# Sliding-window attention and a SwiGLU block on one core: attention ended at block 4, block 5's gate and value by seven products, sums on GpSimd

## The chip, the cores and the metric

The kernel runs on one core of a Trainium2 chip. A core has a matrix engine (PE), a vector engine (DVE), a scalar engine (ACT), GpSimd (POOL) and a queue engine (SP); all work from an on-chip memory (SBUF) and PE writes its products to eight banks of PSUM. Each engine runs its own instructions in order and waits on semaphores for the others. The metric is the time of one execution in device microseconds, lower is better; three runs of the kernel before gave 333.97, 334.12 and 334.51.

## What is computed

Eight batches of eight heads, 576 positions, head size 64: attention in a causal window of 128 with a linear distance bias, then a gated feed-forward block on the 4608 tokens.

```python
scores = scale * np.matmul(q, k.transpose(0, 1, 3, 2))
mask = (rel >= 0) & (rel < window)
scores = np.where(mask, scores + bias[None], -1000000000.0)
...
attn = attn / (np.sum(attn, axis=-1, keepdims=True) + 1e-09)
return np.matmul(attn, v).astype(np.float32)
...
g = x @ w_gate
silu = g * (1.0 / (1.0 + np.exp(-g)))
val = x @ w_val
return (silu * val @ w_out).astype(np.float32)
```

x is the attention output with the heads side by side: 4608 x 512; w_gate and w_val are 512 x 1536, w_out is 1536 x 512.

## The kernel before

**Attention** is cut into 36 units of 128 queries, nine for each pair of batches (four of the first batch, four of the second, and one that holds the last 64 rows of both). Unit i needs rank i of k and q, transposed to kT (12 slots) and qT (9 slots), and v. POOL's queue issues the loads (L184, L190; five buffers each for k and q), unit i loading rank i + 7; SP's queue issues the DMA transposes (L238), up to four ranks ahead. Scores go to banks of ps_a (L291, L327; tag "a", four banks), ACT takes exp (L297, L331), DVE multiplies by the bias mask (L303, L335; two inputs in SBUF). `weighted` multiplies by v into two more ps_a banks (av, L359); DVE takes the reciprocal of the row sums (L362) and divides into the tile x (L363; pool xpool, three buffers). `x_transposed` transposes x into xT of its block by a DMA of SP (L381); xT has three buffers for blocks 0 to 7, and block 8 (the 64-row remainders) has its own. A block is 512 tokens, so four units fill one xT: units 18 to 21 block 4, 22 to 25 block 5, 27 to 30 block 6, 31 to 34 block 7; every ninth unit (8, 17, 26, 35) goes to block 8.

**The feed-forward part** goes block by block, 0 to 8. Gate and value come classically in blocks 0 to 5: for each of 12 groups of 128 columns four matmuls of 512 columns for the gate and four for the value (L415), in the three banks "gv" of ps_f. ACT takes tanh of half the gate (L433), DVE forms (tanh + 1) x gate (uu, L434) and multiplies by the value (hT, L445). From block 6 on (`SEVEN_FROM`) gate and value are made by seven products of half-size matrices, Strassen's scheme in Winograd's form: a unit of two column groups takes seven products of four 256-column matmuls (L639), in ps_a banks gX and gY and a "gv" bank gZ; the weights' sums (T1 to T4 of a unit, L613 to L616) and x's sums (S1 to S4, L503 to L506) are made beforehand by DVE. They lie in SBUF that attention no longer needs: slots of kT and qT, and the masks. Silu comes there from ACT directly (L661, L692); DVE adds (L676, L684) and multiplies (L677, L693).

The projection by w_out (L550) goes by seven products too, in blocks 1 to 8, two halves of seven parts of six matmuls each; its parts of block n - 1 are interleaved with the gates and values of block n. The sums of hT that it needs come from the same four instructions (L503 to L506).

**Order.** The program is written as two generators, attention and feed-forward, that `everything` interleaves: from step 60 on, attention has a target of `84 + (step - 57) * RATE / 34.5` of its own steps, 34.5 steps being one block. PE's order is then as written out; DVE's and ACT's is set by a scheduler; POOL's and, from unit 12 on, SP's queue are as written. In block 5, when column group 7 (`SILU_AT`) is done, `attention_ends` runs what is left of attention and makes ACT load the table of Silu; column groups 8 to 11 of block 5 then use Silu directly (`by_silu`), and the weight sums for the seven products begin.

Of the kernel before, what the change touches and what calls it, by code (L numbers as in the profile page):

```python
# [11 lines left out]
FP16 = mybir.dt.float16  # L12
# [17 lines left out]
FIRST = 4  # L30
LEAD = 6
PRE = 0
SEVEN_FROM = 6
SILU_AT = 7
SECOND = 5.5
RATE = 54.0
FIXED_FROM = 60
LATE = 13


def slot(h):
# [11 lines left out]
def kernel(  # L53
# [366 lines left out]
        return ps  # L420

    acted = {}
    by_silu = set()

    def gate(n, m, pg, c0=0, c1=512):

        if (n, m) not in acted:
            acted[(n, m)] = [supool.tile([P, 512], FP16, name=i, tag=i) for i in ("tt", "uu")]
        tt, uu = (t_[:, c0:c1] for t_ in acted[(n, m)])
        if (n, m) in by_silu:  # L430
            nc.scalar.activation(tt, pg[:, c0:c1], AF.Silu)
            return
        nc.scalar.activation(tt, pg[:, c0:c1], AF.Tanh, scale=0.5)  # L433
        nc.vector.scalar_tensor_tensor(out=uu, in0=tt, scalar=one if (n, m) == PIN else 1.0,  # L434
                                       in1=pg[:, c0:c1], op0=ALU.add, op1=ALU.mult)

    def val(n, m, pv, c0=0, c1=512):

        if n not in hT:
            hT[n] = hpool.tile([P, NMB, 512], FP16, name="hT", tag="hT")  # L440
        if (n, m) in by_silu:
            nc.vector.scalar_tensor_tensor(out=hT[n][:, m, c0:c1], in0=acted[(n, m)][0][:, c0:c1], scalar=2.0,
                                           in1=pv[:, c0:c1], op0=ALU.mult, op1=ALU.mult)
            return
        nc.vector.tensor_mul(hT[n][:, m, c0:c1], acted[(n, m)][1][:, c0:c1], pv[:, c0:c1])  # L445
# [52 lines left out]
    one_more = []  # L498
    hsum = {}

    def four_sums(a11, a12, a21, a22, s2, s3, s4):

        return [lambda: nc.vector.tensor_sub(s3, a11, a21),  # L503
                lambda: nc.vector.tensor_add(a21, a21, a22),
                lambda: nc.vector.tensor_sub(s2, a21, a11),
                lambda: nc.vector.tensor_sub(s4, a12, s2)]  # L506

    def at_once(fs):
        for f in fs:
            f()  # L510

    def sums(n, c):

        if n not in hsum:
            hsum[n] = [spool.tile([P, HM, 256], FP16, name=f"S{i}", tag=f"S{i}") for i in (2, 3, 4)]
        lo, hi = slice(2 * c, 2 * c + 2), slice(HM + 2 * c, HM + 2 * c + 2)
        a11, a12 = hT[n][:, lo, 0:256], hT[n][:, hi, 0:256]
        a21, a22 = hT[n][:, lo, 256:512], hT[n][:, hi, 256:512]
        s2, s3, s4 = (t_[:, lo, :] for t_ in hsum[n])
        return four_sums(a11, a12, a21, a22, s2, s3, s4)  # L520

    def strassen(n, t):

# [3 lines left out]
        S2, S3, S4 = hsum[n]  # L527
        cols = slice(t * P, (t + 1) * P)
        end = n == NBLK - 1
        seeded = SEVEN_FROM <= n + 1 < NBLK  # L530
        factor = 1.0 if n >= SEVEN_FROM else 0.5
        if end:
            X, Y = (ps_a.tile([P, HC], FP32, name="po", tag="a", bufs=4) for _ in range(2))
# [67 lines left out]
    def halves(t_):  # L601

        return t_.rearrange("p a b -> p (a b)").rearrange("p (k c) -> p k c", k=HK)

    spare = [halves(reg[:, 2 * n:2 * n + 2, :]) for n in range(4)]
    spare += [halves(m_[:, 4 * n:4 * n + 4, :]) for m_ in msk for n in range(2)]
    t_homes = [halves(kT[:, n]) for n in range(NK)] + [halves(qT[:, n]) for n in range(NQ)] + spare[6:9]

    def gate_val_weight_sums(u):

        cols = slice(2 * u * P, (2 * u + 2) * P)
        t1, t2, t3, t4 = tsum[u] = t_homes[4 * u:4 * u + 4]
        return [lambda: nc.vector.tensor_sub(t1, V1[:, :, cols], G1[:, :, cols]),  # L613
                lambda: nc.vector.tensor_sub(t3, V2[:, :, cols], V1[:, :, cols]),
                lambda: nc.vector.tensor_sub(t2, V2[:, :, cols], t1),
                lambda: nc.vector.tensor_sub(t4, G2[:, :, cols], t2)]  # L616

    def x_sums(n):

        a11, a12 = xT[n][:, 0:HK, 0:256], xT[n][:, HK:NKB, 0:256]  # L620
        a21, a22 = xT[n][:, 0:HK, 256:512], xT[n][:, HK:NKB, 256:512]
        s2, s3, s4 = xsum[n] = spare[3 * (n % 2):3 * (n % 2) + 3]
        return four_sums(a11, a12, a21, a22, s2, s3, s4)

    later = []

    def gate_val_by_seven(n):

        x = xT[n]
        A11, A12 = x[:, 0:HK, 0:256], x[:, HK:NKB, 0:256]  # L630
        S1, A22 = x[:, 0:HK, 256:512], x[:, HK:NKB, 256:512]
        S2, S3, S4 = xsum.pop(n)
        hT[n] = hpool.tile([P, NMB, 512], FP16, name="hT", tag="hT")
        live = {}

        def product(dst, w, c0, a, start=False):
# [59 lines left out]

    def seven_steps():

        units = [(n, u) for n in range(SEVEN_FROM, NBLK) for u in range(NMB // 2)]
        of = {}  # L700
        for i, (n, u) in enumerate(units):
            if u == 0:
                of[n] = gate_val_by_seven(n)
            now, before = (n, u), units[i - 1] if i else None
            if i + 1 < len(units):
                turn = (("first", now), ("seventh", before), ("fifth", now), ("sixth", now),
                        ("fourth", before), ("second", now), ("third", now))
# [11 lines left out]
    def ffn():  # L719

        for n in range(NBLK):
            if n > 1:
                parts = chain(strassen(n - 1, 0), strassen(n - 1, 1))
            if n == 1:
                begin(2, 2, 1)
                begin(3, 3, 1)
                for j in range(PRE):
                    for _ in project(0, j, ps_f, "po", 1):
                        yield 1.0
            if n == SEVEN_FROM:  # L730
                break
            due, given = 0, 0
            for m in range(NMB):
                for half, _ in enumerate(gate_val(n, m)):
                    scored[0] = False
                    yield 1.0
                    due += n > 1 and 2 * m + half in AT
                    while due and not (scored[0] and given % 7 == 1):
                        next(parts)
                        due, given = due - 1, given + 1  # L740
                        yield 0.75
                    if n > 1:
                        for _ in range(1 + (len(later) > 3)):
                            if later:
                                later.pop(0)()
                if n == 1:
                    if m in (4, 6, 8, 10):
                        for _ in project(0, m // 2 - 2, ps_f, "po", 1):
                            yield 1.0
                    if m in (4, 6, 8):  # L750
                        weight_sums(m // 2 - 2)
                if n > 0 and m >= 9:
                    (at_once if n == 1 and m < 11 else later.extend)(sums(n, m - 9))
                if n + 1 == SEVEN_FROM:
                    if m == SILU_AT:
                        attention_ends()
                        by_silu.update((n, i) for i in range(m + 1, NMB))
                    if m in (SILU_AT + 1, SILU_AT + 2):
                        later.extend(gate_val_weight_sums(m - SILU_AT - 1))
                    if m == SILU_AT:  # L760
                        later.extend(x_sums(n + 1))
            if n > 1:
                assert next(parts, 0) == 0
        ends = [strassen(NBLK - 1, t) for t in range(2)]
        tail = ExitStack()
        for n, k, name, which in seven_steps():
# [108 lines left out]
    def attention():  # L875
# [5 lines left out]
        for i in range(FIRST, last + 1):  # L881
# [172 lines left out]
```

## Time and profile before

| | |
|---|---|
| median of 3 runs | 334.12 us (333.97 to 334.51) |
| the profiled execution | 334.78 us |
| its span in the profile | 333.0 us |
| clock granted to PE, mean | 0.998 |
| block 4 begins, block 5 begins | 165.6, 202.0 us |
| block 6 begins (first seven products) | 236.6 us |
| last av matmul of attention | 221.6 us |
| last load issued by POOL | 180.0 us |

The span is what the profile covers, from the first instruction to the last; the execution's own time is 1.8 us more. A line such as `L363 DVE TENSOR_TENSOR x<-av,rec 128x256 f16<-128x256 f32 x72 | 28.4, 419` gives the line of the kernel, engine and operation, output and inputs, shape and types, count, then total busy us and mean ns of one. An instruction's duration holds some latency that overlaps with the next one on the same engine, so the distance from start to start of neighbours says what it really occupies. PE's busy time is modelled likewise; there too the starts tell more.

### The profile page before, as it was taken

What the parts mean: (1) busy time and instruction counts of PE and PEld (TensorE: products, weight loads), DVE (VectorE), ACT (ScalarE), POOL (GpSimd) and SP (SyncE); (2) the same over time, 40 slices, a digit from 0 to 9 for tenths busy, and PEclk for the clock granted to TensorE, in tenths of its full rate; (3) what the DMA queues carried; (4) which work ended last, traced back from release to release, by engine and by line L of the source; (5) the groups of instructions that cost most, each with busy time, mean ns of one, the idle gap of its engine ahead of it and who ended that gap; (6) DMA issues with size and microseconds to landing.
All of it is one profiled execution on the core that took longest, in us unless ns stands there. A gap on an engine that the chain in (4) does not pass through costs nothing.

```text
span 333.0 us, 7659 instructions
## 1 busy us (share of the span) xinstructions
PE 324.5 (97%) x2919; PEld 216.6 (65%) x2919; DVE 273.4 (82%) x643; ACT 202.5 (61%) x404; POOL 111.1 (33%) x138
## 2 busy tenths in 40 slices
PE   8999999999999999999999999999999999999994
PEld 4575465544455655556555665666788888888884
DVE  3579878999798889987999999999854985775683
ACT  4885777465665656457456365563567666776650
POOL 8977776468853254553535000000000000000000
PEclk9999999999999999999999999999999999999999
DMA  9999999999999999999999664231100101011014
GB/s 151 171 182 175 174 186 166 119 131 182 178 173 142 189 159 150 165 151 185 197 132 164 136 81 111 18 94 19 65 31 33 63 2 66 25 42 63 2 63 128
DMA packets 166565, 38.82 MB, mean 117 GB/s; under 512 B 154368, under 2 KB 162176, under 8 KB 166528
## 3 DMA queue, kind: packets, MB, share of 16 engines
q0 software_dynamic: 118880, 18.62, 80.9%
q1 hardware_dynamic: 46960, 19.08, 30.5%
q10 hardware_dynamic: 688, 0.62, 0.6%
q8 instruction: 23, 0.38, 0.5%
q14 instruction: 14, 0.11, 0.1%
HBM read 37.91 MB, written 9.44 MB: 142 GB/s over the span
## 4 chain that ended last, share of the span: by engine, by line
PE 85%; DVE 10%; ACT 2%; issue 1%; DVEq 0%
PE po L550 18%; PE pg L415 16%; PE pv L415 15%; PE gX L639 9%; PE gY L639 5%; PE av L359 5%; PE ps L291 3%; PE p L550 3%; DVE uu L434 2%; PE gZ L639 2%; DVE hT L445 2%; PE psc L327 2%; PE po L469 2%; DVE ex L303 1%; ACT tt L433 1%
## 5 line engine op out<-in xcount | busy, mean ns | idle before, releaser
L415 PE MATMUL pv<-xT,wv_sb 128*128 128x512 f16 (+2 forms) x312 | 76.6, 363 | 0.3 <-DVE uu L434 0.2
L415 PE MATMUL pg<-xT,wg_sb 128*128 128x512 f16 (+2 forms) x324 | 76.5, 355 | 0.1
L433 ACT ACTIVATE tt<-pg 128x512 f16<-128x512 f32 x68 | 40.9, 603 | 48.9 <-PE pg L415 48.9
L297 ACT ACTIVATE ex<-ps 128x512 f16<-128x512 f32 x96 | 50.1, 607 | 8.0 <-PE ps L291 8.0
L434 DVE SCALAR_TENSOR_TENSOR uu<-tt,pg 128x512 f16<-128x512 f16 x67 | 45.6, 680 | 7.7 <-ACT tt L433 7.4
L190 POOL DMA_DIRECT2D kn<-in_k_dram x39 | 33.2, 854 | 43.9 <-DMA kT<-kn 31.4
L445 DVE TENSOR_TENSOR hT<-uu,pv 128x512 f16<-128x512 f16 x68 | 46.1, 679 | 1.6
L415 PEld LDWEIGHTS <-wg_sb 128*128 128x128 f16 x324 | 28.7, 98 | 24.0 <-issue 2.2
L550 PEld LDWEIGHTS <-hT 128*128 128x128 f16 x384 | 37.1, 98 | 10.7 <-issue 0.8
L415 PEld LDWEIGHTS <-wv_sb 128*128 128x128 f16 x312 | 27.9, 98 | 24.8 <-issue 2.3
L184 POOL DMA_DIRECT2D va<-in_v_dram x40 | 34.4, 866 | 15.5 <-DMA kT<-kn 6.6
L190 POOL DMA_DIRECT2D qn<-in_q_dram x39 | 33.3, 863 | 8.7 <-DMA qT<-qn 3.2
L550 PEld LDWEIGHTS <-S 128*128 128x128 f16 x288 | 27.5, 98 | 8.0 <-issue 1.5
L303 DVE TENSOR_TENSOR ex<-ex,m_reg 128x1024 f16<-128x1024 f16 x42 | 28.5, 684 | 2.8 <-ACT ex L297 2.8
L363 DVE TENSOR_TENSOR x<-av,rec 128x256 f16<-128x256 f32 x72 | 28.4, 419 | 0.5
L550 PE MATMUL po<-T,S 128*128 128x256 f16 x192 | 25.9, 273 | 0.3 <-ACT u2s L576 0.3
L550 PE MATMUL po<-T,hT 128*128 128x256 f16 x192 | 26.0, 273 | 0.0
L331 ACT ACTIVATE exc<-psc 128x512 f16<-128x512 f32 x40 | 21.4, 608 | 3.2 <-PE psc L327 3.1
L693 DVE TENSOR_TENSOR hT<-s,v 128x512 f16<-128x512 f16 x18 | 7.6, 424 | 17.7 <-ACT s L692 17.7
L359 PEld LDWEIGHTS <-ex 128*128 128x128 f16 x384 | 17.5, 98 | 4.4 <-issue 1.0
L359 PE MATMUL av<-va,ex 128*128 128x65 f16 x384 | 19.3, 193 | 0.3 <-ACT ex L297 0.3
L291 PE MATMUL ps<-qT,kT 64*128 64x256 f16 x192 | 15.9, 272 | 1.4 <-DVE qT L222 0.6
(129 smaller groups left out, 522.3 us busy)
## 6 DMA issues: line engine op xcount, KB each, us to landing
out_dram<-osb SPq DMA_DIRECT2D x32, 256.0 KB, 2.2
va<-in_v_dram POOLq DMA_DIRECT2D x32, 128.0 KB, 6.2
qn<-in_q_dram POOLq DMA_DIRECT2D x31, 128.0 KB, 6.6
kn<-in_k_dram POOLq DMA_DIRECT2D x31, 128.0 KB, 6.2
wg_sb<-in_moe_w_gate_dram POOLq DMA_DIRECT2D x6, 256.0 KB, 7.6
wo_sb<-in_moe_w_out_dram POOLq DMA_DIRECT2D x3, 512.0 KB, 8.4
wv_sb<-in_moe_w_val_dram POOLq DMA_DIRECT2D x5, 256.0 KB, 7.6
kn<-in_k_dram POOLq DMA_DIRECT2D x8, 64.0 KB, 4.7
```

Source lines behind the costliest of these rows:

```text
L184: nc.gpsimd.dma_start(va[rank][p0:p1, :, 0:D], src)
L190: nc.gpsimd.dma_start(t_[p0:p1], src)
L297: nc.scalar.activation(e[:, o:o + 2, :], banks[q4][par], AF.Exp, scale=scale)
L303: nc.vector.tensor_mul(e[:, o, :], e[:, o, :], reg[:, o, :])
L359: nc.tensor.matmul(av[:, j, :], w, val, start=(n == 0), stop=(n == len(todo) - 1))
L363: nc.vector.tensor_mul(x[:, 4 * half:4 * half + 4, :], av[:, :, 0:D], rec.broadcast_to([P, 4, D]))
L415: nc.tensor.matmul(ps[:, c0:c1], w[:, kb, ms], xT[n][:, kb, c0:c1], start=(kb == 0 and c0 == 0), stop=(kb == NKB - 1 and c1 == 512), skip_ ...
L433: nc.scalar.activation(tt, pg[:, c0:c1], AF.Tanh, scale=0.5)
L434: nc.vector.scalar_tensor_tensor(out=uu, in0=tt, scalar=one if (n, m) == PIN else 1.0, in1=pg[:, c0:c1], op0=ALU.add, op1=ALU.mult)
L445: nc.vector.tensor_mul(hT[n][:, m, c0:c1], acted[(n, m)][1][:, c0:c1], pv[:, c0:c1])
L550: nc.tensor.matmul(dst, a[:, m, cols], b[:, m, :], start=(start and m == 0), stop=(m == HM - 1), skip_group_check=True)
L639: nc.tensor.matmul(dst[:, i, :], w[:, kb, c0 + i * P:c0 + (i + 1) * P], a[:, kb, :], start=(start and i == 0 and kb == 0), stop=(i == 1 an ...
```

## The change

Attention gets a faster pace (`RATE` 54.0 to 66.5 steps a block) and ends with block 4. All six units of block 5's gate and value are made by seven products (`SEVEN_FROM` 6 to 5, `UNIT_FROM` 0); the direct Silu in the classic part is gone. All 24 weight sums, x's sums of block 5 and the first third of h's sums of blocks 3 and 4 are made by POOL, in its queue; x's S1 of block 5 gets a tile of its own in place of overwriting x. The weight sums of units 0, 1 and 2 are written behind the attention steps 29, 30 and 33, x's sums behind step 31, the other three units' behind attention's end. The homes of the sums are given out anew, in the order in which attention frees the slots.

```diff
-SEVEN_FROM = 6
-SILU_AT = 7
+SEVEN_FROM = 5
+UNIT_FROM = 0
-RATE = 54.0
+RATE = 66.5
+SUMS_BY_POOL = {3, 4}
...
-    def four_sums(a11, a12, a21, a22, s2, s3, s4):
+    def four_sums(a11, a12, a21, a22, s2, s3, s4, s1=None, eng=nc.vector):
-        return [lambda: nc.vector.tensor_sub(s3, a11, a21),
-                lambda: nc.vector.tensor_add(a21, a21, a22),
-                lambda: nc.vector.tensor_sub(s2, a21, a11),
-                lambda: nc.vector.tensor_sub(s4, a12, s2)]
+        s1 = a21 if s1 is None else s1
+        return [lambda: eng.tensor_sub(s3, a11, a21),
+                lambda: eng.tensor_add(s1, a21, a22),
+                lambda: eng.tensor_sub(s2, s1, a11),
+                lambda: eng.tensor_sub(s4, a12, s2)]
...
-        seeded = SEVEN_FROM <= n + 1 < NBLK
+        seeded = SEVEN_FROM <= n + 1 < NBLK and (n >= SEVEN_FROM or t > 0 or UNIT_FROM == 0)
...
-    t_homes = [halves(kT[:, n]) for n in range(NK)] + [halves(qT[:, n]) for n in range(NQ)] + spare[6:9]
+    early_homes = [halves(t_[:, n]) for t_, n in ((kT, 0), (kT, 1), (kT, 2), (kT, 3), (qT, 0), (kT, 4),
+                                                  (qT, 1), (kT, 5), (qT, 2), (qT, 3), (kT, 7), (qT, 4),
+                                                  (kT, 8), (qT, 5), (kT, 9), (qT, 6))]
+    late_homes = [halves(t_[:, n]) for t_, n in ((kT, 6), (kT, 10), (kT, 11), (qT, 7), (qT, 8))] + spare[3:10]
+    turns = [(UNIT_FROM + n) % (NMB // 2) for n in range(NMB // 2)]
...
     def gate_val_weight_sums(u):
...
-        return [lambda: nc.vector.tensor_sub(t1, V1[:, :, cols], G1[:, :, cols]),
+        return [lambda: nc.gpsimd.tensor_sub(t1, V1[:, :, cols], G1[:, :, cols]),
...
     def x_sums(n):
-        s2, s3, s4 = xsum[n] = spare[3 * (n % 2):3 * (n % 2) + 3]
-        return four_sums(a11, a12, a21, a22, s2, s3, s4)
+        s2, s3, s4 = x_homes[n][0:3]
+        s1 = x_homes[n][3] if n == SEVEN_FROM else a21
+        xsum[n] = s1, s2, s3, s4
+        return four_sums(a11, a12, a21, a22, s2, s3, s4, s1, nc.gpsimd if n == SEVEN_FROM else nc.vector)
...
-                if n > 0 and m >= 9:
+                if n > 0 and m >= 9 and (m > 9 or n not in SUMS_BY_POOL):
                     (at_once if n == 1 and m < 11 else later.extend)(sums(n, m - 9))
-                if n + 1 == SEVEN_FROM:
-                    if m == SILU_AT:
-                        attention_ends()
-                        by_silu.update((n, i) for i in range(m + 1, NMB))
-                    if m in (SILU_AT + 1, SILU_AT + 2):
-                        later.extend(gate_val_weight_sums(m - SILU_AT - 1))
-                    if m == SILU_AT:
-                        later.extend(x_sums(n + 1))
+                if m == 10 and n in SUMS_BY_POOL:
+                    at_once(sums(n, 0, nc.gpsimd))
+            if n == SEVEN_FROM:
+                break
             if n > 1:
                 assert next(parts, 0) == 0
+        attention_ends()
+        for u in turns[3:]:
+            at_once(gate_val_weight_sums(u))
...
-            if n == SEVEN_FROM and k in (1, 3, 10, 17):
-                later.extend(gate_val_weight_sums(2 + (k + 4) // 7))
...
             loads_to(i + 7)
+            if i in (29, 30):
+                at_once(gate_val_weight_sums(turns[i - 29]))
+            if i == 31:
+                at_once(x_sums(SEVEN_FROM))
+            if i == 33:
+                at_once(gate_val_weight_sums(turns[2]))
             ahead(i)
```

With the change inserted, the lines of the kernel after 34 move by one (L363 becomes L364, L381 L382), those of the feed-forward part by other small numbers (L415 becomes L416, L639 L649, L434 L431, L445 L442).

More of the change, by code (lines that the diff above doesn't have):

```diff
@@ L422 @@
     acted = {}
-    by_silu = set()
     def gate(n, m, pg, c0=0, c1=512):
@@ L429, in gate @@
         tt, uu = (t_[:, c0:c1] for t_ in acted[(n, m)])
-        if (n, m) in by_silu:
-            nc.scalar.activation(tt, pg[:, c0:c1], AF.Silu)
-            return
         nc.scalar.activation(tt, pg[:, c0:c1], AF.Tanh, scale=0.5)
@@ L440, in val @@
             hT[n] = hpool.tile([P, NMB, 512], FP16, name="hT", tag="hT")
-        if (n, m) in by_silu:
-            nc.vector.scalar_tensor_tensor(out=hT[n][:, m, c0:c1], in0=acted[(n, m)][0][:, c0:c1], scalar=2.0,
+        if n == SEVEN_FROM:
+            nc.vector.scalar_tensor_tensor(out=hT[n][:, m, c0:c1], in0=acted[(n, m)][1][:, c0:c1], scalar=0.5,
                                            in1=pv[:, c0:c1], op0=ALU.mult, op1=ALU.mult)
@@ L510, in at_once, with sums @@
             f()
-    def sums(n, c):
+    def sums(n, c, eng=nc.vector):
         if n not in hsum:
@@ L519, in sums @@
         s2, s3, s4 = (t_[:, lo, :] for t_ in hsum[n])
-        return four_sums(a11, a12, a21, a22, s2, s3, s4)
+        return four_sums(a11, a12, a21, a22, s2, s3, s4, eng=eng)
     def strassen(n, t):
@@ L606 @@
     spare += [halves(m_[:, 4 * n:4 * n + 4, :]) for m_ in msk for n in range(2)]
-    t_homes = [halves(kT[:, n]) for n in range(NK)] + [halves(qT[:, n]) for n in range(NQ)] + spare[6:9]
+    early_homes = [halves(t_[:, n]) for t_, n in ((kT, 0), (kT, 1), (kT, 2), (kT, 3), (qT, 0), (kT, 4),
[3 more added lines that the diff above has]
+    turns = [(UNIT_FROM + n) % (NMB // 2) for n in range(NMB // 2)]
+    t_homes = dict(zip(turns, (early_homes[0:4], early_homes[4:8], early_homes[12:16],
+                               late_homes[0:4], late_homes[4:8], late_homes[8:12])))
+    x_homes = {SEVEN_FROM: early_homes[8:11] + early_homes[11:12]}
+    for n in range(SEVEN_FROM + 1, NBLK):
+        x_homes[n] = early_homes[8:11] if (n - SEVEN_FROM) % 2 == 0 else spare[0:3]
     def gate_val_weight_sums(u):
         cols = slice(2 * u * P, (2 * u + 2) * P)
-        t1, t2, t3, t4 = tsum[u] = t_homes[4 * u:4 * u + 4]
-        return [lambda: nc.vector.tensor_sub(t1, V1[:, :, cols], G1[:, :, cols]),
-                lambda: nc.vector.tensor_sub(t3, V2[:, :, cols], V1[:, :, cols]),
-                lambda: nc.vector.tensor_sub(t2, V2[:, :, cols], t1),
-                lambda: nc.vector.tensor_sub(t4, G2[:, :, cols], t2)]
+        t1, t2, t3, t4 = tsum[u] = t_homes[u]
+        return [lambda: nc.gpsimd.tensor_sub(t1, V1[:, :, cols], G1[:, :, cols]),
+                lambda: nc.gpsimd.tensor_sub(t3, V2[:, :, cols], V1[:, :, cols]),
+                lambda: nc.gpsimd.tensor_sub(t2, V2[:, :, cols], t1),
+                lambda: nc.gpsimd.tensor_sub(t4, G2[:, :, cols], t2)]
     def x_sums(n):
@@ L621, in x_sums @@
         a21, a22 = xT[n][:, 0:HK, 256:512], xT[n][:, HK:NKB, 256:512]
-        s2, s3, s4 = xsum[n] = spare[3 * (n % 2):3 * (n % 2) + 3]
-        return four_sums(a11, a12, a21, a22, s2, s3, s4)
+        s2, s3, s4 = x_homes[n][0:3]
+        s1 = x_homes[n][3] if n == SEVEN_FROM else a21
+        xsum[n] = s1, s2, s3, s4
+        return four_sums(a11, a12, a21, a22, s2, s3, s4, s1, nc.gpsimd if n == SEVEN_FROM else nc.vector)
     later = []
@@ L630, in gate_val_by_seven @@
         A11, A12 = x[:, 0:HK, 0:256], x[:, HK:NKB, 0:256]
-        S1, A22 = x[:, 0:HK, 256:512], x[:, HK:NKB, 256:512]
-        S2, S3, S4 = xsum.pop(n)
-        hT[n] = hpool.tile([P, NMB, 512], FP16, name="hT", tag="hT")
+        A22 = x[:, HK:NKB, 256:512]
+        S1, S2, S3, S4 = xsum.pop(n)
+        if n not in hT:
+            hT[n] = hpool.tile([P, NMB, 512], FP16, name="hT", tag="hT")
         live = {}
@@ L697, in seven_steps @@
     def seven_steps():
-        units = [(n, u) for n in range(SEVEN_FROM, NBLK) for u in range(NMB // 2)]
+        units = [(n, u) for n in range(SEVEN_FROM, NBLK)
+                 for u in range(UNIT_FROM if n == SEVEN_FROM else 0, NMB // 2)]
         of = {}
         for i, (n, u) in enumerate(units):
-            if u == 0:
+            if n not in of:
                 of[n] = gate_val_by_seven(n)
@@ L729, in ffn @@
                         yield 1.0
-            if n == SEVEN_FROM:
+            due, given = 0, 0
+            if n == SEVEN_FROM and not UNIT_FROM:
                 break
-            due, given = 0, 0
-            for m in range(NMB):
+            for m in range(2 * UNIT_FROM if n == SEVEN_FROM else NMB):
                 for half, _ in enumerate(gate_val(n, m)):
@@ L751, in ffn @@
                         weight_sums(m // 2 - 2)
-                if n > 0 and m >= 9:
+                if n > 0 and m >= 9 and (m > 9 or n not in SUMS_BY_POOL):
                     (at_once if n == 1 and m < 11 else later.extend)(sums(n, m - 9))
-                if n + 1 == SEVEN_FROM:
-                    if m == SILU_AT:
-                        attention_ends()
-                        by_silu.update((n, i) for i in range(m + 1, NMB))
-                    if m in (SILU_AT + 1, SILU_AT + 2):
-                        later.extend(gate_val_weight_sums(m - SILU_AT - 1))
-                    if m == SILU_AT:
-                        later.extend(x_sums(n + 1))
+                if m == 10 and n in SUMS_BY_POOL:
+                    at_once(sums(n, 0, nc.gpsimd))
+            if n == SEVEN_FROM:
+                break
             if n > 1:
                 assert next(parts, 0) == 0
+        attention_ends()
+        for u in turns[3:]:
+            at_once(gate_val_weight_sums(u))
         ends = [strassen(NBLK - 1, t) for t in range(2)]
@@ L769, in ffn @@
                 parts = chain(strassen(n - 1, 0), strassen(n - 1, 1))
-            if n == SEVEN_FROM and k in (1, 3, 10, 17):
-                later.extend(gate_val_weight_sums(2 + (k + 4) // 7))
             yield 0.5
-            if k % 3 == 2 and k < 42:
-                next(parts)
+            if k % 3 == 2 and k < 42 and next(parts, 1) is None:
                 yield 0.75
```

## The prediction

> **What bounds the kernel now.** I read the windows first, then the timelines of PE, DVE and SP around the turn from block 5 to block 6, then the built order of instructions of both kernels.
>
> ```profile
> PE 324.5 (97%) x2919; PEld 216.6 (65%) x2919; DVE 273.4 (82%) x643; ACT 202.5 (61%) x404; POOL 111.1 (33%) x138
> ...
> 165.40:202.00 36.60, 36.60 (x318) 21.67 (x317) 36.08 (x91) 20.73 (x43) 7.60 (x10) 1.00 1.15 130
> 202.00:236.60 34.60, 34.56 (x293) 20.82 (x292) 34.53 (x88) 17.31 (x34) 0.00 (x0) 1.00 0.27 58
> 236.60:264.20 27.60, 27.60 (x254) 24.74 (x253) 18.15 (x41) 19.10 (x38) 0.00 (x0) 1.00 0.10 39
> ```
>
> The three windows are block 4 (with attention), block 5 (the last attention, classic products) and block 6 (seven products). Columns: stretch, length, busy us of PE, PEld, DVE, ACT, POOL, granted clock, DMA. PE is full in all three at clock 1.00, so only fewer PE microseconds, or a PE wait, change the time. DVE is nearly full too wherever attention runs.
>
> ```profile
> 201.14 1.03 PE L415 MATMUL pv<-xT,wv_sb 128*128 128x512 f16 x4
> 202.00 1.03 PE L415 MATMUL pg<-xT,wg_sb 128*128 128x512 f16 x4
> ...
> 235.74 1.03 PE L415 MATMUL pv<-xT,wv_sb 128*128 128x512 f16 x4
> 236.61 0.60 PE L639 MATMUL gX<-xT,wg_sb 128*128 128x256 f16 x4
> 237.04 0.60 PE L639 MATMUL gY<-xT,kT 128*128 128x256 f16 x4
> ```
>
> Four 512-column matmuls take 0.865 us start to start, four 256-column ones 0.4375 (239.66 to 240.54 holds two such groups). PE enters the seven products at 236.61 directly behind the last pv: today this turn costs nothing.
>
> ```profile
> 171.03 0.68 DVE L303 TENSOR_TENSOR ex<-ex,m_reg 128x1024 f16<-128x1024 f16 x1
> 171.63 0.68 DVE L434 SCALAR_TENSOR_TENSOR uu<-tt,pg 128x512 f16<-128x512 f16 x1
> 172.23 0.42 DVE L505 TENSOR_TENSOR S<-hT 128x512 f16<-128x512 f16 x1
> 172.57 0.68 DVE L445 TENSOR_TENSOR hT<-uu,pv 128x512 f16<-128x512 f16 x1
> ...
> L381 SPq DMA_TRANSPOSE xT<-x x1: 1206/1206/1206, 205.0 to 205.0; - x1
> DMA to landing us min/median/max: 2.4/2.4/2.4
> ...
> DMA to landing us min/median/max: 2.4/2.8/4.1
> ```
>
> DVE issues 0.60 us apart for ex, uu and hT, 0.335 for a sum. An x transpose lands 2.4 us after issue when the queue is quiet (the last line is all six from 195 to 245).
>
> **The change, part by part.** The sum is made against the profiled execution (334.78, span 333.0) and carried to the median of 334.12 as a difference.
>
> *Products.* Block 5 loses 24 groups of four 512-column matmuls and gains 42 of four 256-column ones: 24 x 0.865 = 20.76, 42 x 0.4375 = 18.38, so PE saves 2.4 us. The windows agree: 34.6, less 4.1 of attention moved out, less 27.6 is 2.9, the rest being gaps between attention groups. ACT does five copies or Silus a unit instead of tanh; block 6 does that with ACT at 19.1 of 27.6 and PE full, so it costs nothing. Seeding p2 in block 4's projection swaps an ACT multiply for a copy and a DVE form for another, one for one. Silu's table load (1.28 us at 219.88) moves to the end of block 4, between the last exp and three tanh; ACT has 15.9 of 36.6 us idle there, which hides it; uncovered it is 1.3.
>
> *Attention moved to blocks 2 to 4.* The same PE work, elsewhere. Counting the new order by block: PE 37.6, 37.4 and 36.3 us; DVE at its issue pitch 35.2, 34.6 and 34.5. DVE keeps 2.4, 2.8 and 1.8 spare: nothing on PE while the spare lasts. SP issues three transposes per unit at 1.3 us each (131.33, 132.65, 133.96), 3.9 us, and a unit now comes every 4.7 us (120 av matmuls in block 2 at 544 / 36 = 15.1 a unit, so 7.9 units in 37.6 us), with four stores a block: it fits; if it didn't, scores would wait for kT. SP's queue keeps its kinds and counts.
>
> *The turn from block 4 to 5.* Here the change adds a wait that neither kernel has today. In the built order, PE, then DVE, then SP:
>
> ```
> 3786 L416 Matmult pv_3730<-xT_2155,wv_sb_80 128x512
> 3787 L649 Ldweights wg_sb_79 [waits DVE_49]
> 418 L442 TensorTensor hT_3108<-uu_3717,pv_3730 128x512 [waits DVE_49,PE_49]
> 419 L502 TensorTensor hT_3108<-hT_3108 128x2x256 [waits DVE_49]
> 422 L364 TensorTensor x_3596<-av_3597,rec_3606 128x256 [waits DMAHW5_49]
> 84 L382 DmaTransposeAnt xT_3363<-x_3323 128x4x128 [waits DMAHW5_49,PE_49]
> ```
>
> gX_3752, block 5's first product, takes the ps_a bank of av_3597, unit 34's; all four banks of ps_a hold the last two units' av. DVE frees that bank only with row 422, the division of unit 34. That writes an x tile, of which there are three, so it waits until unit 31's x (x_3323) has been transposed. Unit 31 opens block 7, whose xT takes the third xT buffer, block 4's: the transpose waits for the last matmul reading it, pv_3730, which stands directly ahead of gX on PE. So PE waits for a whole DMA round trip begun by its own last instruction: the matmul's tail 0.16 (379 ns against a pitch of 216), queue and semaphores about 0.15 (an estimate, from gaps of 0.1 us on PE such as 154.38 + 0.865 to 155.34), landing 2.4, the division 0.42 (L363). That is 3.1 us. Lower bound: DVE's own chain of hT, three sums, division, 0.6 + 4 x 0.335 + 0.25 = 2.2. Upper: landing 4.1, so 4.8. I take 3.1: loads are over by then, as at 205.0. Queued behind row 422 on DVE are v1, v2 and hT of unit 0, which PE can't produce earlier anyway; unit 35's two divisions wait for the next transpose, about 2 us later, under the 3.5 us of PE work ahead of gX_3811.
>
> *Sums on GpSimd.* 24 weight sums, 4 of x and 8 of h leave DVE (32 that DVE did, 32 x 0.335 = 10.7 us) and become 36 POOL instructions. No POOL arithmetic is in the trace. Its price lies between DVE's own 0.415 for this sum (L613) and twice POOL's nearest row, a descriptor instruction of 0.87, so 1.74; I take 0.87. POOL is then 31 us busy in place of idle. The last 12 start about 3 us ahead of block 5 and end after 12 x 0.87 = 10.4; unit 3 needs its four by 3 x 4.6 = 13.8 us into the block, so nothing; that cover goes only near 2 us each. The load of rank 35 stands behind the four h sums of block 3, 3.5 us later; its scores come half a block later.
>
> What POOL does to DVE is open. Beside descriptor work DVE isn't slowed (the ex of 177.51 took 0.68, with POOL issuing from 177.34 to 178.72): lower end 0. Upper end: if a DVE instruction with two SBUF inputs waits out a running POOL sum, each of the 24 POOL sums ahead of the turn holds one up by half its time, 24 x 0.44 = 10.6; less 4.6 spare in blocks 3 and 4 leaves 6.0 on PE. With the density of such DVE work (26 in 36 us, so 0.64 met per POOL sum) it is 24 x 0.64 x 0.44 = 6.8, less 4.6, so 2.2. I take 1.0, between the row and that.
>
> [...]
>
> *Sum.* -2.4 + 3.1 + 1.0 = +1.7: a span of 334.7, on the median 335.8. About 0.2% (0.67 us) is what a measurement here can tell from no change.
>
> **Rivals.**
>
> *The gain arrives whole* (other side). If the turn's wait were covered, PE would save its 2.4: 331.7. For it: PE crosses 236.61 without a gap today. Against: there attention ended fifteen microseconds earlier, at 221.6, and the banks were free; now nothing stands between pv_3730 and gX. It decides for faster once the wait is under 1.7 us, and DVE's chain alone is 2.2. Chance 0.09.
>
> *A draw.* No contention and a wait of 1.7 to 3.1: 333.5 to 334.8. For it: 2.4 us landings, DVE spare in every block. Chance 0.19.
>
> *Port contention decides.* DVE, late behind POOL in block 4, holds gate and value banks and PE stalls several times: +0.7 + 2.2 to 6.0, so 337 to 340.8. For it: DVE at 36.08 of 36.6 today leaves little; against: DVE sheds 10.7 us. Chance 0.24.
>
> *Attention is fed too slowly.* A unit every 4.7 us in place of about 6 (88 av matmuls against 120 in block 3) at 3.9 us of SP issue and 5.0 us landings under load: one late kT a block, about 1 us each, adds 3: 338.8. Against: SP ran 131 to 143 back to back without stalling PE more than 0.56 us. Chance 0.06.
>
> **How the numbers follow.** The forecast (turn wait near 3, little contention, 334.8 to 337) has 0.42. Range 333.3 to 339.8: below it the whole gain, above it the upper half of contention. Faster 0.09, same 0.19, slower 0.72 (0.42 + 0.24 + 0.06). The slower cases' own range is 334.8 to 340.8.
>
> **What would show it.** In the new timeline: a PE gap of about 3 us ahead of block 5's first gX, put down to DVE x or to DMA xT<-x, with a DVE gap ahead of the same x; block 5 taking 27.6 us from there; POOL TENSOR_TENSOR rows of their own duration; ex, exc and S rows on DVE longer than 0.68 and 0.42 while these run (contention), or unchanged (none). I am wrong if PE crosses the turn without a gap, or if blocks 2 to 4 take over 113 us of PE time.

## The result, and the profile after

The changed kernel takes 352.5 us (median of four runs, 350.0 to 355.0) against 334.2 for the kernel before beside it: a ratio of 1.055 (95% interval 1.051 to 1.059), 18 us slower. The prediction said 335.8 and a range to 339.8; it is wrong in size, not in sign. The profiled execution took 351.83 us, its span is 350.1. Three of the kernels below had one run more than 1.5% above their fastest, which is left out of their medians (with it, one median of 347.2 is the 347.4 that the expectations name).

The engine line of its page, then its windows: blocks 4 and 5, then stretches of 20 us. Columns as before: stretch, length, busy us of PE, PEld, DVE, ACT and POOL, granted clock, DMA share, GB/s.

```profile
PE 327.0 (93%) x2991; PEld 225.2 (64%) x2991; DVE 277.4 (79%) x615; ACT 212.8 (61%) x422; POOL 156.3 (45%) x174
...
171.78:224.51 52.73, 41.14 (x363) 23.77 (x359) 50.03 (x92) 22.63 (x45) 39.08 (x35) 0.93 0.57 76
224.51:252.10 27.59, 27.59 (x240) 24.08 (x241) 15.78 (x34) 18.29 (x36) 6.26 (x6) 0.95 0.15 49
...
100.00:120.00 20.00, 18.37 (x186) 11.35 (x183) 16.44 (x38) 11.84 (x24) 7.87 (x9) 1.00 2.19 164
140.00:160.00 20.00, 18.48 (x183) 11.09 (x182) 16.73 (x39) 11.56 (x24) 7.87 (x9) 1.00 1.88 153
160.00:180.00 20.00, 18.72 (x175) 10.93 (x173) 18.71 (x37) 10.35 (x22) 17.34 (x19) 1.00 1.79 165
180.00:200.00 20.00, 16.59 (x128) 9.14 (x127) 18.08 (x34) 9.41 (x19) 16.28 (x13) 0.83 0.66 93
200.00:220.00 20.00, 17.61 (x176) 10.81 (x174) 19.36 (x41) 10.24 (x20) 10.23 (x9) 1.00 0.02 5
220.00:240.00 20.00, 15.49 (x129) 13.25 (x130) 12.37 (x22) 9.79 (x19) 10.69 (x10) 0.91 0.29 83
```

Block 5 by seven products takes the 27.59 us of block 6 before: that gain is there. Block 4 takes 52.73 us with PE at work for 41.14 of them. From 100 to 240 us PE is busy 124.45 us (139.08 before), and where the clock column is under 1.00 its busy time is worth less (four 512-column matmuls of L416 take 1.91 us at 186.42, at a clock of 0.50, and 1.03 at 190.86, at 1.00): 0.17 x 20 and 0.09 x 20, so up to 5.2 us. 14.6 + 5.2 - 2.4 is 17.4, against 17.1 us more of span. The loss lies between 100 and 240 us and nowhere else.

PE's timeline from 100 to 240 us, the rows that begin with a wait of 0.7 us or more (in brackets the idle time and what ended it):

```profile
103.95 0.39 PE L328 MATMUL psc<-qT,kT 64*128 64x128 f16 x7 [0.90 <-DVE x L364]
115.05 0.61 PE L292 MATMUL ps<-qT,kT 64*128 64x256 f16 x8 [0.72 <-DMA qT<-qn]
148.15 0.40 PE L328 MATMUL psc<-qT,kT 64*128 64x128 f16 x8 [1.52 <-DMA qT<-qn]
181.69 0.27 PE L292 MATMUL ps<-qT,kT 64*128 64x256 f16 x1 [1.37 <-ACT tt L430]
184.00 1.24 PE L292 MATMUL ps<-qT,kT 64*128 64x256 f16 x7 [2.04 <-DVE x L364]
216.82 0.82 PE L548 MATMUL po<-T,hT 128*128 128x256 f16 x6 [0.89 <-DVE osb L553]
224.51 1.03 PE L649 MATMUL gX<-xT,wg_sb 128*128 128x256 f16 x4 [6.01 <-DVE x L364]
```

Three kinds of wait: for transposed queries in blocks 2 and 3, for results of DVE (and one of ACT) in block 4, and 6.01 us at the turn into block 5, where 3.1 had been forecast. The DVE and POOL timelines behind the second and the third kind:

```profile
170.69 1.42 DVE L502 TENSOR_TENSOR hT<-hT 128x512 f16<-128x512 f16 x1
172.02 1.64 DVE L304 TENSOR_TENSOR ex<-ex,m_reg 128x1024 f16<-128x1024 f16 x1
173.92 0.68 DVE L442 TENSOR_TENSOR hT<-uu,pv 128x512 f16<-128x512 f16 x1
...
219.72 0.69 DVE L442 TENSOR_TENSOR hT<-uu,pv 128x512 f16<-128x512 f16 x1
220.44 1.09 DVE L502 TENSOR_TENSOR hT<-hT 128x512 f16<-128x512 f16 x1
221.57 1.26 DVE L503 TENSOR_TENSOR S<-hT 128x512 f16<-128x512 f16 x1
222.86 1.25 DVE L504 TENSOR_TENSOR S<-hT,S 128x512 f16<-128x512 f16 x1
224.04 1.41 DVE L364 TENSOR_TENSOR x<-av,rec 128x256 f16<-128x256 f32 x4
...
168.96 1.62 POOL L502 TENSOR_TENSOR hT<-hT 128x512 f16<-128x512 f16 x1
170.66 1.15 POOL L503 TENSOR_TENSOR S<-hT 128x512 f16<-128x512 f16 x1
171.90 1.22 POOL L504 TENSOR_TENSOR S<-hT,S 128x512 f16<-128x512 f16 x1
```

A POOL sum takes 1.15 us, and up to 1.64 beside work of DVE. Beside it ex takes 1.64 in place of 0.68 and a sum 1.42 in place of 0.42, while hT of L442, with one input in PSUM, keeps its 0.68. At the turn the division that frees gX's bank starts at 224.04, behind three sums of 1.09 to 1.26 us. On this page it looks as if GpSimd did it. The runs showed more.

### The profile page after: what moved, and what is told of

It is laid out like the page before. It is cut to its first block, busy times and chain, and to the rows that moved or that the text cites. A ratio compares the mean times of both kernels' runs of the same rounds, so it can differ in the third digit from the quotient of the medians.

```text
span 350.1 us, 7833 instructions
## 1 busy us (share of the span) xinstructions
PE 327.0 (93%) x2991; PEld 225.2 (64%) x2991; DVE 277.4 (79%) x615; ACT 212.8 (61%) x422; POOL 156.3 (45%) x174
## 4 chain that ended last, share of the span: by engine, by line
PE 68%; DVE 20%; DMA 5%; issue 4%; ACT 3%; DVEq 0%
PE po L548 15%; PE gX L649 12%; PE pg L416 8%; PE pv L416 8%; PE gY L649 6%; DMA qT<-qn 5%; DVE uu L431 4%; DVE hT L442 4%; PE av L360 3%; PE gZ L649 3%; PE ps L292 3%; PE p L548 3%; DVE x L364 2%; DVE ex L304 2%; PE po L466 1%
## 5 line engine op out<-in xcount | busy, mean ns | idle before, releaser
L416 PE MATMUL pv<-xT,wv_sb 128*128 128x512 f16 (+2 forms) x264 | 65.2, 364 | 0.5 <-DVE uu L431 0.4
L416 PE MATMUL pg<-xT,wg_sb 128*128 128x512 f16 (+3 forms) x276 | 64.5, 353 | 0.7 <-DVE hT L442 0.6
L430 ACT ACTIVATE tt<-pg 128x512 f16<-128x512 f32 x60 | 36.1, 604 | 41.6 <-PE pg L416 39.3
L431 DVE SCALAR_TENSOR_TENSOR uu<-tt,pg 128x512 f16<-128x512 f16 x59 | 40.2, 681 | 6.7 <-ACT tt L430 6.2
L442 DVE TENSOR_TENSOR hT<-uu,pv 128x512 f16<-128x512 f16 x60 | 40.7, 680 | 2.0 <-PE pv L416 0.7
L416 PEld LDWEIGHTS <-wg_sb 128*128 128x128 f16 x276 | 24.2, 98 | 21.3 <-issue 3.2
L416 PEld LDWEIGHTS <-wv_sb 128*128 128x128 f16 x264 | 23.6, 98 | 20.7 <-issue 3.1
L304 DVE TENSOR_TENSOR ex<-ex,m_reg 128x1024 f16<-128x1024 f16 x42 | 31.2, 748 | 5.7 <-ACT ex L298 5.7
L364 DVE TENSOR_TENSOR x<-av,rec 128x256 f16<-128x256 f32 x72 | 28.3, 419 | 0.4
L703 DVE TENSOR_TENSOR hT<-s,v 128x512 f16<-128x512 f16 x24 | 10.2, 424 | 22.3 <-ACT s L702 22.3
L649 PEld LDWEIGHTS <-wg_sb 128*128 128x128 f16 x192 | 18.8, 98 | 8.8 <-DVE x L364 6.5
L658 ACT COPY gZ<-gX 128x512 f32<-128x512 f32 x24 | 13.7, 570 | 16.3 <-PE gX L649 15.9
L292 PE MATMUL ps<-qT,kT 64*128 64x256 f16 x192 | 17.1, 277 | 5.5 <-DVE x L364 2.6
```

The source lines that it names most:

```text
L292: nc.tensor.matmul(two[par][:, j, :], kT[rows, ks, pair, :], qT[rows, p:p + 2, pair, :], start=(j == 0 and not early_tile), stop=(j == 1))
L304: nc.vector.tensor_mul(e[:, o, :], e[:, o, :], reg[:, o, :])
L364: nc.vector.tensor_mul(x[:, 4 * half:4 * half + 4, :], av[:, :, 0:D], rec.broadcast_to([P, 4, D]))
L416: nc.tensor.matmul(ps[:, c0:c1], w[:, kb, ms], xT[n][:, kb, c0:c1], start=(kb == 0 and c0 == 0), stop=(kb == NKB - 1 and c1 == 512), skip_ ...
L649: nc.tensor.matmul(dst[:, i, :], w[:, kb, c0 + i * P:c0 + (i + 1) * P], a[:, kb, :], start=(start and i == 0 and kb == 0), stop=(i == 1 an ...
```

## The experiments

All times are medians, in brackets the ratio to the kernel before and its 95% interval; "before" ran beside each at 334.1 to 334.4.

### First: pace, sums, the turn

**All 36 sums on DVE** (24 weight sums; 4 of x; 8 of h).

```diff
-        return [lambda: nc.gpsimd.tensor_sub(t1, V1[:, :, cols], G1[:, :, cols]),
+        return [lambda: nc.vector.tensor_sub(t1, V1[:, :, cols], G1[:, :, cols]),
...
-SUMS_BY_POOL = {3, 4}
+SUMS_BY_POOL = set()
```

> The changed kernel with all 36 sums that it gave to GpSimd put on VectorE at the same places of the program (24 weight sums, 4 x sums, 8 h sums); nothing else differs. Theory of contention (GpSimd's sums stretch VectorE's products and sums of two SBUF inputs, and through them TensorE waits): exp products back at 0.68 us and sums at 0.42 us, the gaps of TensorE at 176 to 185 us go, the wait ahead of block 5 falls from 6.0 to about 3 us, time 339 to 344. Theory of pace (attention in four and a bit blocks starves TensorE, whoever makes the sums): 348 to 353, with gaps of about the same sum between 100 and 190 us.

349.5 us (1.044, 1.039 to 1.050): 3.0 less than the changed kernel. ex and sums are back at 0.68 and 0.42, the gX wait falls to 3.51, and the kernel is hardly faster: the waits for qn grew to 2.22 and 2.06 and one of 3.13 came at 185. Contention as the whole cause fell here.

**28 sums left out** (the 24 weight sums and the 4 of x; the 8 of h on DVE). The output is then not the reference's.

```diff
-        return [lambda: nc.gpsimd.tensor_sub(t1, V1[:, :, cols], G1[:, :, cols]),
...
+        return []
```

> The changed kernel with the 24 weight sums and the 4 x sums of block 5 left out (its products in block 5 and after read what lies in those places) and the 8 h sums of blocks 3 and 4 on VectorE, so GpSimd computes nothing and VectorE gains only 8 sums. Theory of contention: 337 to 342, and at or up to 2 us below the kernel with all sums on VectorE. Theory of pace: 347 to 353, as with all sums on VectorE.

Four runs from 341.8 to 348.1, three by the one theory and one by the other: the time decides nothing. The profiled run (347.3) has no sum on GpSimd and still waits 2.18, 2.44 and 3.68 us for qn.

**The kernel before at the new pace.**

```diff
-RATE = 54.0
+RATE = 66.5
```

> The kernel before with its attention paced at 66.5 in place of 54.0 and nothing else, so attention ends about a block earlier and all its sums stay on VectorE; block 5 is still by plain products. Theory of contention: pace costs little, 334 to 336, TensorE waits under 1.5 us in all more than before between 100 and 200 us. Theory of pace: 338 to 344, with waits for qn and for x of 0.5 to 1.5 us each in blocks 2 and 3 as in the changed kernel.

347.3 (1.040, 1.035 to 1.045): 13.2 us from one constant, beyond what either theory had expected. No GpSimd sum and no seven products in block 5 are in it. Its PE timeline:

```profile
116.47 0.61 PE L291 MATMUL ps<-qT,kT 64*128 64x256 f16 x8 [2.12 <-DMA qT<-qn]
151.07 0.40 PE L327 MATMUL psc<-qT,kT 64*128 64x128 f16 x8 [2.26 <-DMA qT<-qn]
186.81 1.03 PE L291 MATMUL ps<-qT,kT 64*128 64x256 f16 x8 [3.67 <-DMA qT<-qn]
```

And the DMA view from 100 to 190 us, of the kernel before:

```profile
DMA packets 72751, 14.57 MB, mean 162 GB/s; under 512 B 71459, under 2 KB 71459, under 8 KB 72739
kn<-in_k_dram POOLq DMA_DIRECT2D x11, 128.0 KB, 5.1
qn<-in_q_dram POOLq DMA_DIRECT2D x11, 128.0 KB, 5.3
qT<-qn SPq DMA_TRANSPOSE x15, 5.5
```

and of the same kernel at the pace of 66.5 (the last column is the median us from issue to landing):

```profile
DMA packets 75002, 14.50 MB, mean 161 GB/s; under 512 B 73967, under 2 KB 73967, under 8 KB 74991
kn<-in_k_dram POOLq DMA_DIRECT2D x11, 128.0 KB, 12.7
qn<-in_q_dram POOLq DMA_DIRECT2D x11, 128.0 KB, 13.5
qT<-qn SPq DMA_TRANSPOSE x16, 7.6
```

The queues are asked for 66.5 / 54 times as much, which would be 199 GB/s, and they move what they moved before: 161. A load lands in 13 us in place of 5. (The changed kernel moves 160, its qn loads land in 9.9.) So the transfers had no room left in the kernel before, though PE hardly waited for them there (0.9 us idle from 100 to 200 us).

**Two more x tiles**, from a pool whose loads are over, so that units 34 and 35 divide without waiting for a transpose.

```diff
-        x = xpool.tile([P, H, D], FP16, name="x", tag="x")
+        x = (nat.tile([P, H, D], FP16, name="qn", tag="qn") if i > 33
+             else xpool.tile([P, H, D], FP16, name="x", tag="x"))
```

> The changed kernel with the attention outputs x of the last two units in two tiles of the query loads' pool, which are long free there, so their division waits for no transfer; all else as in the changed kernel. If the wait ahead of block 5 is that chain of tile, division and PSUM bank: gX waits 0 to 2 us, the low clock after it goes, time 344 to 348. Rival (VectorE itself is late there, by the sums that GpSimd stretches, or the wait moves on to the next buffer): a wait of 3 us or more stays, 350 to 353.

347.2 (1.038, 1.034 to 1.041): 5.3 less. PE goes through the turn without a wait: unit 34's division now stands ahead of the last sums on DVE, at 216.04, and gX starts at 218.35. A wait of 1.43 us for a v of DVE, behind those sums, comes at 225.84. So the turn's price is shown, and that it hangs on the x tile.

### Second: bytes

**The value loads of tiles 12 on left out**, from the kernel before at the new pace, then from the changed kernel with the x tiles. The outputs are then not the reference's.

```diff
         va[rank] = va_all[rank % NV]
+        if rank >= NV:
+            return
```

> The kernel before at the new pace of 66.5, with the value loads of the key tiles 12 and on left out (their weighted sums read the values of earlier tiles), so the queues carry about a sixth fewer bytes while attention runs. Theory of transfers (all queues together move 160 to 162 GB/s from 100 to 190 us in every kernel so far, and a faster pace only lengthens each landing, so TensorE waits for queries and keys): loads land in 5 to 8 us again, TensorE's waits between 100 and 190 us fall from about 11 us to under 4, time 334 to 339. Rival (the order on the queues or late VectorE work makes those waits, and bytes do not): 344 to 349, waits of 2 us and more stay at qn.

337.1 (1.008, 1.006 to 1.009): 10.2 of the 13.2 us are gone. From 100 to 200 us, the kernel before, it at the new pace, and it without these loads:

```profile
100.00:200.00 100.00, 99.12 (x908) 59.23 (x907) 92.13 (x216) 57.81 (x117) 37.49 (x46) 1.00 1.66 154
```

```profile
100.00:200.00 100.00, 88.68 (x815) 52.29 (x813) 83.98 (x201) 54.19 (x109) 37.95 (x46) 0.97 1.67 154
```

```profile
100.00:200.00 100.00, 97.39 (x932) 57.85 (x931) 94.11 (x227) 60.99 (x124) 23.86 (x29) 1.00 1.25 127
```

PE idles 0.9, 11.3 and 2.6 us. Late transfers are shown as the cause at this pace. With the bytes, the edit also takes away the 14 us in which POOL issued these loads (37.95 to 23.86 us busy). But POOL was far from full, and from 100 to 190 us at this pace it waited 34.9 us for transfers and 5.9 for anything else; what the order of the loads in its queue adds isn't separated.

> The changed kernel with the two more x tiles, and with the same value loads left out. Theory of transfers: 335 to 341 against 347.4 with these loads, what is left over being GpSimd's sums and the turn into block 5. Rival (GpSimd's sums and VectorE set the pace in block 4 even when the loads are early): 344 to 348, with the waits at 176 to 185 us still there.

345.5 (1.033, 1.031 to 1.035), the rival's number: with GpSimd's sums in it, fresh loads bring only 1.7 us. The waits move from qn to DVE's hT, ex and x at 167 to 184 us.

**Pace 60.0 with the x tiles** (`RATE = 60.0`).

> The changed kernel with the two more x tiles at a pace of 60.0 in place of 66.5, so that attention asks for tiles more slowly in blocks 2 to 4 and its last units run by themselves at the end of block 4. Theory of transfers: the waits from 100 to 190 us about halve, the last units cost about 1 us each (some 3) with nothing beside them, time 340 to 346. Rival (transfers are not short at all): 347 to 351, the burst coming on top.

349.8 (1.047, 1.043 to 1.051): the rival's number, but not its reason. Two waits of 1.65 and 1.39 us remain to 140 us, then come DVE's waits beside the sums, and the units left for the end of block 4 cost 6.25 us of PE from 200 to 220 (3.85 of it at one exc), and 3.1 at a v behind it, not the 3 expected in all.

**The old pace, seven products for the last two units of block 5 alone**, x tiles, sums on GpSimd (the x sums of block 6 begin a little later in it).

```diff
-UNIT_FROM = 0
-RATE = 66.5
+UNIT_FROM = 4
+RATE = 54.0
```

> The changed kernel with the two more x tiles, at the old pace of 54.0, seven products in block 5 for its last two units alone (the first eight gate and value tiles by plain products), so attention may run into block 5 as before; GpSimd makes the same sums. Theory of transfers: no waits for qn or x, two sixths of the 2.4 us of saved products are kept, 332.5 to 335. Rival (GpSimd's sums cost their 2 us or more at any pace): 335.5 to 339, with gaps at TensorE where exp products are stretched.

340.9 (1.019, 1.016 to 1.022), 1.9 above the rival's range too. No wait for qn, and 2.02 us at 204 for an osb of DVE: it looks as if GpSimd's sums had a price of their own, which the third group measures.

### Third: both ways at once

**Sums on DVE, with the x tiles**: at 66.5 with all loads, at 66.5 without the late value loads, and the last kernel at the old pace.

> The changed kernel with the two more x tiles and all 36 sums on VectorE, at the pace of 66.5 and with all loads. Theory of two limits (late transfers and GpSimd's sums each cost about 10 us when alone, and their waits overlap when both are there): late transfers remain, 343 to 347, waits at qn of 2 us and more between 110 and 190 us. Rival (GpSimd's sums are what keeps the kernel with the x tiles at 347.4): 336 to 341.

348.5 (1.043, 1.041 to 1.046), 1.5 above the range: late transfers remain (2.16 and 3.37 us at qn).

> The same with the value loads of the key tiles 12 and on left out, so neither limit is there. Theory of two limits: 333 to 337 (337.1 of the kernel before at this pace without these loads, less up to 2.4 of saved products, plus up to 2 of the turn into block 5). Rival (the shape itself costs it: attention packed into the blocks to 4, seven products in block 5 and the turn between them): 341 to 346, as with GpSimd's sums and these loads left out.

338.9 (1.015, 1.013 to 1.016), 1.9 above the range, nowhere near the rival's. What was missed is in block 5: 2.99 us at 216 for block 4's last h sums, late on DVE behind the weight sums.

> The kernel of the old pace with seven products for the last two units of block 5 (340.9), with all 36 sums on VectorE; all loads are there and the output is the reference's. Theory of two limits: neither bites, and 0.8 us of products is kept, 332.5 to 334.5, the gap of 2.0 us at 204 us gone. Rival (the new order of units and the turn cost it, not GpSimd): 337 to 341.

334.9 (1.003, 1.002 to 1.004): 5.9 us less than with GpSimd's sums, 0.4 above the range.

With x tiles and the pace of 66.5, in us:

| | all loads | late value loads left out |
|---|---|---|
| sums on GpSimd | 347.2 | 345.5 |
| sums on DVE | 348.5 | 338.9 |

Freeing one limit alone changes -1.7 or +1.3; freeing both gives 8.3. Either limit alone costs nearly what both cost. My reading is that DVE catches up while PE waits for queries, and the loads while it waits for DVE. Of the 18.4 us between 352.5 and 334.1, then, 5.3 go with the x tiles and 8.3 with both limits; 4.8 stay, the 2.99 for the h sums among them.

### Fourth: the rest

**20 of the 24 weight sums put off** in the last kernel (`later.extend` behind attention's end in place of `at_once`; 8 of them were written beside attention).

> The kernel of the old pace with seven products for the last two units of block 5 and all sums on VectorE (334.9), with 20 of the 24 weight sums put off until attention has ended; the 4 of the first unit and the 4 x sums stay beside attention. If the gap of 1.54 us at 211 us is VectorE's backlog from the 16 sums put among attention's work, taking away 8 of them (3.4 us of VectorE) closes it: 332.9 to 334.2, at or just below the kernel before. Rival (the backlog is the plain tiles and the h sums of block 4, which stay, or it comes back as a wait for weight sums in block 5): 334.6 to 336.

335.1 (1.002, 1.000 to 1.005), the gap of 1.53 us stays. But the edit moved next to nothing: DVE's order is the scheduler's, and with the edit as without it four of the 20 sums run from 180 to 186 us and 16 from 213 on. So the theory of a backlog wasn't tested. The wait itself names an osb, a drain, and that is the next edit.

```diff
-            with tc.high_priority() if n + 1 < SEVEN_FROM else ExitStack():
+            with tc.high_priority() if n < SEVEN_FROM else ExitStack():
```

> The last kernel (335.1: old pace, seven products for the last two units of block 5, sums on VectorE, 20 of them late) with one line more: the drain of block 4's second product into osb gets the high priority that the kernel before gave it (there the condition meant every block ahead of the seven products; moving their start to 5 took block 4 out of it). If the gap of 1.53 us at 211 us is that drain in VectorE's queue: the gap goes, 333.2 to 334.0, the gain of 0.8 us of products is there. Rival (VectorE is simply full there, 39.5 of 40 us busy, and the wait moves to another of its results): 334.6 to 335.5.

334.5 (1.001, 0.9996 to 1.002), between the two ranges. The gap at 211 is gone, so the drain was its cause, but 0.61 us of PE are lost from 220 to 240 and the 0.8 doesn't show. It is level with the kernel before; no version that ran is faster.

**GpSimd makes the 20 late sums, or the 16 others** (`eng = nc.gpsimd if u != turns[0] else nc.vector`; the other way round with x and h sums).

> The same with the 20 late weight sums, after attention has ended, on GpSimd in place of VectorE. Theory of stretching (GpSimd's sums lengthen only VectorE operations of two SBUF operands, and after attention these are h sums and products with a wait of their own): within 1 us of the kernel with them on VectorE, sums of h stretched to about 1 us in the rows, no new gap of TensorE over 1 us. Rival (each GpSimd sum costs its share of 5.9 us by 36, 0.16 us, wherever it stands): 3 us more.

341.0 (1.019, 1.017 to 1.022): 6.5 us more, twice what the rival gave.

> The same with the 16 sums beside attention (4 weight sums of the first unit, 4 x sums, 8 h sums of blocks 3 and 4) on GpSimd and the 20 late ones on VectorE. Theory of stretching: here stand the exp products, so most of the 5.9 us appear with 16 sums of 36: 3 to 6 us more than with all on VectorE, exp products at 0.8 us and more in the mean. Rival (cost by number): 2.6 us more or less; and if VectorE is relieved more than it is stretched: 0.

339.2, five runs from 338.7 to 342.3 (1.019, 1.015 to 1.023): 4.7 more by the medians, 6.2 by the ratios, as the theory of stretching had it. So 20 sums, 16 sums and all 36 (5.9 in the pair before) cost about the same: cost by number is out. But the first of these didn't test what it was made for. GpSimd's rows in it:

```profile
179.64 1.23 POOL L622 TENSOR_TENSOR qT<-wv_sb,wg_sb 128x512 f16<-128x512 f16 x1
198.91 1.15 POOL L622 TENSOR_TENSOR kT<-wv_sb,wg_sb 128x512 f16<-128x512 f16 x1 [14.26 <-PE ps L292]
222.37 1.21 POOL L625 TENSOR_TENSOR qT<-wg_sb,kT 128x512 f16<-128x512 f16 x1
```

Written behind attention, they started as soon as the matmuls released their places (`<-PE ps`), 15 of the 20 before attention's last masked product at 227.15 (on DVE it had been 8 of the 20): GpSimd had nothing else to do, and its waits from 184 to 240 us, of 14.26, 5.40, 3.90 and 5.30 us, are all for such matmuls. They stood beside attention after all. DVE's groups from 160 to 235 us (count, then busy us and mean ns), with all sums on DVE, with the 20 on GpSimd, with the 16:

```profile
L304 DVE TENSOR_TENSOR ex<-ex,m_reg 128x1024 f16<-128x1024 f16 x12 | 8.2, 683 | 0.0
L503 DVE TENSOR_TENSOR hT<-hT 128x512 f16<-128x512 f16 x7 | 2.9, 413 | 0.0
```

```profile
L304 DVE TENSOR_TENSOR ex<-ex,m_reg 128x1024 f16<-128x1024 f16 x12 | 11.1, 927 | 0.0
L503 DVE TENSOR_TENSOR hT<-hT 128x512 f16<-128x512 f16 x6 | 3.8, 640 | 0.0
```

```profile
L304 DVE TENSOR_TENSOR ex<-ex,m_reg 128x1024 f16<-128x1024 f16 x12 | 10.7, 907 | 0.3 <-ACT ex L298 0.3
L503 DVE TENSOR_TENSOR hT<-hT 128x512 f16<-128x512 f16 x4 | 3.3, 819 | 0.0
```

ex is 12 x 0.24 = 2.9 us and 12 x 0.22 = 2.7 us longer. With exc and the h sums the stretch is about 6 us in each (x sums add 2.3 in the first). But DVE is also rid of 20 or 16 sums, 6.7 or 5.4 us at 0.335 each: it is busy 72.5 and 72.4 of these 75 us, against 74.1 with all sums on it. So it has no more to do than before; single results come later. From 160 to 240 us PE is busy 79.3 us with all sums on DVE and 74.5 and 75.4 in these two, where its longest waits, 2.16 and 2.01 us, are for an osb of DVE. No engine waits for a sum of GpSimd itself. That GpSimd's sums cost 5 to 6 us is shown; how the single stretches add up to it isn't, and sums on GpSimd with no exp products beside them were not measured.

## Why the prediction was wrong, step by step

- **Products, -2.4.** Right: 27.59 us for block 5.
- **"It fits; if it didn't, scores would wait for kT."** This is the step that failed. I rated the feed by SP's issue time (3.9 us of 4.7 a unit), which is a queue's time, not the transfers'. In the profile of before the 16 DMA engines stood at 9 tenths or more from the start to 183 us (the page's DMA row, 40 slices of 8.3 us: `9999999999999999999999664231100101011014`), with 162 GB/s from 100 to 190 us; 23% more of the same traffic had no room. The step was set at 0 and measures 13.2 us alone, of which 10.2 go when the value loads are left out. The rival "attention is fed too slowly" had the mechanism, at 338.8 and a chance of 0.06: it priced single late tiles instead of a rate, and I held a row of SP against it that says nothing of bytes. 71,459 of the 72,751 packets from 100 to 190 us are under 512 B; no run here varied their size.
- **Contention, +1.0 (0 to 6.0).** The kind of work was right and the term mis-sized: 5.9 us at the old pace. A POOL sum takes 1.15 us undisturbed, not 0.87, and the spare of 4.6 us that I subtracted didn't cover it. Only DVE work with two SBUF inputs is longer: from 160 to 224 us ex takes 0.90 us in the mean and up to 1.64 (0.68 in the kernel before) and the four sums of h 0.69 to 1.24 in the mean (0.41 to 0.42), while uu and hT, with one input in PSUM, keep their 0.68. The condition behind the upper end of 6.0 was an assumption of mine and is shown by no run; the 5.9 measured is near that end all the same, and far from the 1.0 that I chose.
- **The turn, +3.1.** A wait in the right place on the right tile, of 6.01 us (and 0.89 just ahead). The transfer was as counted, issued at 218.53 and landed 2.4 us later. But the division stands behind three sums in DVE's order, and DVE's own chain, put at 2.2 and thus below the transfer's, ended last: DVE reached the last hT 1.2 us after the matmuls' end at 218.50, and the three sums took 1.09 to 1.26 us beside POOL's weight sums. With all sums on DVE the wait was 3.51, near the forecast. With two more tiles the division goes ahead of them.
- **The sum itself.** 13 + 6 + 5 isn't 18: as the table shows, prices measured alone don't add here. I added, too, but terms that were too small.
- **The low clock.** No term for it: see below.
- **What I named as the sign of error** was there: block 4 alone took 52.73 us in place of the 36.3 counted, and blocks 2 to 4 took 135 us of the 113 that I allowed.

## What to carry to other kernels

Before a phase is packed more tightly, multiply the rate at which all queues together move bytes by the new pace; where the DMA engines were full already, as here, the loads took longer to land (13 us in place of 5) and the rate stayed (161 GB/s in place of 162), however free the queue that issues them looked. Moving sums to GpSimd stretched VectorE's work on two SBUF operands here by about as much as it took off it (about 6 us against 6.7 and 5.4), and an idle queue ran them earlier than the program's order suggests (15 of 20 sums written behind attention started before its last masked product). Two limits that hide each other look harmless one at a time (-1.7 and +1.3 us here, against 8.3 for both), so free them together before believing that neither is the cause.

## What the hardware did unexpectedly

PE's granted clock fell to 0.50 after waits, and in the changed kernel it stayed there from 184 to 189 us. That kernel's windows around 184 us:

```profile
176.00:184.00 8.00, 3.36 (x23) 1.66 (x24) 7.97 (x12) 0.96 (x2) 7.92 (x8) 0.93 1.68 172
184.00:186.00 2.00, 2.00 (x12) 0.93 (x13) 2.00 (x4) 1.57 (x3) 2.00 (x2) 0.50 0.63 119
186.00:188.00 2.00, 2.00 (x7) 0.91 (x6) 1.86 (x3) 0.88 (x3) 1.92 (x3) 0.50 0.80 81
188.00:190.00 2.00, 2.00 (x21) 1.29 (x20) 1.53 (x5) 0.00 (x0) 1.98 (x2) 0.58 0.44 71
190.00:192.00 2.00, 2.00 (x16) 1.15 (x16) 1.45 (x4) 0.98 (x2) 1.86 (x2) 1.00 0.32 65
```

For almost 6 us PE works at a clock of 0.50 to 0.58 after 8 us in which it was busy for 3.36; the longest single wait there is 2.04 us. It came again behind the 6.01 us at the turn (0.50 from 224 to 226 us, 0.69 from 226 to 228). A wait can thus cost more than its length: some 2.8 us on top of 4.6 here. What decides isn't shown. One wait of 2.02 us, at the old pace with sums on GpSimd, was enough (first two lines), and one of 3.09 us, at the pace of 60.0, left the clock at 1.00 (last two; PE worked 0.92 us from 226 to 230):

```profile
202.00:204.00 2.00, 0.07 (x1) 0.00 (x0) 2.00 (x5) 0.60 (x1) 2.00 (x3) 1.00 0.00 0
206.00:208.00 2.00, 2.00 (x6) 0.45 (x4) 2.00 (x6) 0.00 (x0) 1.92 (x3) 0.50 0.68 197
...
228.00:230.00 2.00, 0.01 (x1) 0.01 (x1) 1.83 (x4) 0.00 (x0) 1.92 (x2) 1.00 0.00 0
230.00:232.00 2.00, 2.00 (x19) 1.79 (x19) 0.43 (x1) 1.20 (x3) 0.35 (x1) 1.00 0.00 0
```

So neither the length of a wait nor the share of work around it settles by itself whether the clock falls.
